# Query projections and key sums of two batches as one stretch of float32 products

## The chip, the cores and the metric

The kernel runs on one core of a Trainium2 chip. The metric is the device time of one execution in microseconds; smaller is better. TensorE (PE in the profile) multiplies matrices into PSUM, VectorE (DVE) and ScalarE (ACT) work elementwise and read PSUM, GpSimd (POOL) works on SBUF only, and SyncE (SP) issues all DMAs here. Each engine runs its instructions strictly in the order in which the program lists them.

## The reference

For each of 4 batches (4 heads, 1088 positions, head size 32) an attention with product features feeds a gated feed-forward block with a product over the positions. Everything is float32.

```python
def phi(x):                                   # S1, S2: 8 x 32
    a = einsum('rd,bhsd->bhsr', S1, x)
    b = einsum('rd,bhsd->bhsr', S2, x)
    return einsum('bhsi,bhsj->bhsij', a, b)   # 64 features a position and head
q_p, k_p = phi(q), phi(k)
kv = einsum('bhsf,bhsd->bhfd', k_p, v); z = k_p.sum(axis=2)    # sums over the keys
x = einsum('bhsf,bhfd->bhsd', q_p, kv) / (einsum('bhsf,bhf->bhs', q_p, z) + 1e-6)
h = relu(x @ w_in); u, v = h[..., :512], h[..., 512:]
v_n = (v - mean(v)) / sqrt(var(v) + 1e-6)
out = (u * (einsum('ts,bsd->btd', w_spatial, v_n) + b_spatial)) @ w_out
```

## The kernel before, in words

**Arithmetic.** The large products run as three passes on pairs of a high and a low part (type float32r, helper `mm3` at L444 to L446; `high` and `low` at L969, L971, L978 and L980). The small products of the attention run as plain float32: the projections of the keys (`project`, L593), the projections of the queries (`proj`, L733) and the sums over the keys (`part` in `keys`, L630). The profile shows a float32 product as two instructions. So a query group is 4 instructions (two halves of 192 or, in the last group, 160 columns), the keys of a batch are 36 with 64 columns, and the sums are 144 with 33 columns. The projections write 64 columns of the array, the sums 32.

**A batch's attention** (`attention(b)`, batches 1 to 3 counted from 0; batch 0 has its own path). Three query groups are loaded (`qt`, tag `c`), projected into a PSUM bank of tag `sd` each (`pab`), copied by ACT to `abT` (L737), written to DRAM (`qd`, L740) and read back in broadcast form (L744, L747) into `fa` and `fb` (tag `pl`); POOL multiplies these to query features (L748), which ACT and POOL split (tag `r`, L457). Meanwhile the keys are projected into two `sd` banks (`kab`); ACT copies one half to `ka` (L598) and DVE makes key features `kp` (L600), three buffers. The sums multiply those with the loaded values into another `sd` bank (`kv`), which DVE spreads to `kd` (L758) and ACT and DVE split to `kvh`, `kvl`. Then, for each of three groups: the numerators and denominators (`nd`, L775, three passes a piece), a reciprocal on DVE (L779), the attention's output `xh`, `xl`, and `hidden_v`, the half of the hidden layer that is normalised (`pv`, L799; tag `sd` again). Tag `sd` has two banks, and each tag hands out its buffers in the order in which the program creates the tiles. So the next batch's first projection follows the last `pv` of the batch before.

**Order of the work.** `main(b)` (hidden layer, product over the positions, output) and `attention(b + 1)` are interleaved by a planner: each operation has a planned cost and a due time worked back from the dues of what needs it, shifted by a table of corrections by name (`LEADS`). Among what could start in the planner's own clock, it takes the earliest due. `TURN = 125` is the planner's charge, in ns, for each change between float32 and float32r products (the flag `f4`). The planner yields one fixed order for each engine; on the chip, semaphores alone decide when an instruction starts. The last stage is `main(3)` with `quad`, which saves products by forming sums first.

Of the kernel before, what the change touches and what calls it, by code (L numbers as in the profile page):

```python
# [17 lines left out]
B, H, S, D, R = 4, 4, 1088, 32, 8  # L18
DM, DFF, DH = 128, 1024, 512
P = 128  # L20
# [12 lines left out]
TW = (384, 384, 320)  # L33
# [30 lines left out]
AFTER = (0, 35.0, 0, 0)  # L64
# [6 lines left out]
AFTER_T = 200.0  # L71
LAST = B - 1, ND - 1, 0
TAIL = (0, 212), (212, 212)

ON_ACT = ()
ADD_UP = 187
TURN = 125

SLACK = {'PE': 32, 'ACT': 56, 'DVE': 106, 'POOL': 890, 'SP': 84}

FILL_COLD, COLD_TO = 460, 7000
FILL, FILL_TO, FILL_SPARE = 224, 50.0, 150
FIRST_RATE, LOW_DELAY = 0.18, 4.4
# [50 lines left out]
class Order:  # L134
# [75 lines left out]
    def schedule(self):  # L210
# [31 lines left out]
        while left:  # L242
# [47 lines left out]
            if e == "PE":  # L290

                s += TURN * (o.f4 != f4)
                f4 = o.f4
# [56 lines left out]
def c_act(n, psum=False, ptr=False):  # L350
    return (157 if psum else 190) + 0.833 * n + (190 if ptr else 0) if n > 16 else 203
# [19 lines left out]
def tile_kernel(ctx: ExitStack, tc: tile.TileContext, kT, qT, vA, sks, idn, msk, wT, w_in, w_out, bsp, out):  # L371
# [6 lines left out]
    nc = tc.nc  # L378
# [57 lines left out]
    k = Order(place)  # L436
    k.whole = lambda tag: homes[tag].rearrange("p n c -> p (n c)")
    op, tl = k.op, k.tile

    def bank(tag, name):  # L440
        return tl(tag, name, [P, 512])
# [6 lines left out]
    def load(t, ap, src, kb, w=None, **kw):  # L448
        if t.name in FIRST:
            kw["due"] = FIRST.index(t.name) - 1e4  # L450
        op("SP", 470, lambda: nc.sync.dma_start(out=ap(), in_=src), w=[w or t], kb=kb, **kw)
# [9 lines left out]
    z9 = tl("u", "z9", [P, P])  # L461
# [3 lines left out]
    wps = bank("sd", "wps")  # L465
# [9 lines left out]
    eps = tl(None, "eps", [P, 2])  # L475
# [9 lines left out]
    NSK = 2 * H * R  # L485
# [44 lines left out]
    sk = tl(None, "sk", [P, 2 * NSK])  # L530
    s_raw = tl("pl", "s_raw", [P, 384])
# [5 lines left out]
    mask = tl(None, "mask_sb", [P, 2])  # L537
    load(mask, lambda: mask.ap, msk, 1)

    kd0 = tl("u", "kd0", [P, 2, 2, D + 1])  # L540

    wTh = tl(None, "wTh", [P, NS, ROW], F32R)
    wTl = tl(None, "wTl", [P, NS, ROW], F32R)
    wih = tl(None, "wih", [P, DFF], F32R)
    wil = tl(None, "wil", [P, DFF], F32R)
    woh = tl(None, "woh", [P, ND, DM], F32R)
    wol = tl(None, "wol", [P, ND, DM], F32R)
# [41 lines left out]
    def project(ab, xt, at=0):  # L589

        for t in range(3):
            for j in range(2):
                nc.tensor.matmul(ab_view(ab, at)[64 * j:64 * j + 64, :, t], xt[:, t * P + 64 * j:t * P + 64 * j + 64], sk[:, :NSK], start=True, stop=True)  # L593
# [19 lines left out]
    def keys(b):  # L613

        xts, vs = [], []
        for g in range(3):
            xt = tl("kt", f"kt{b}{g}", [P, 384])
            load(xt, lambda xt=xt, g=g: xt.ap, kT[b, g], 192, after=AFTER[b])
            v_sb = tl("v", f"v{b}{g}", [P, 3, H * (D + 1)])
            load(v_sb, lambda v_sb=v_sb: v_sb.ap.rearrange("p t c -> p (t c)"), vA[b, g], 198, after=AFTER[b])  # L620
            xts.append(xt)
            vs.append(v_sb)
        kv = bank("sd" if b else "pu", f"kv{b}")

        def part(g, f):
            for t in range(3):
                for pr in range(2):
                    for q in range(4):
                        c, h = 128 * pr + 32 * q, 2 * pr + q // 2
                        nc.tensor.matmul(  # L630
                            kv[32 * q:32 * q + 32, pr * (D + 1):(pr + 1) * (D + 1)], f[:, t, c:c + 32], vs[g][:, t, h * (D + 1):(h + 1) * (D + 1)],
                            start=(g == 0 and t == 0 and pr == 0), stop=(g == 2 and t == 2 and pr == 1), tile_position=(0, 32 * q),
                        )

        if not b:
            for g in range(3):
                f = phi(b, g, xts[g], "k")
                op("PE", 410, f4=True, fn=lambda g=g, f=f: part(g, f), r=[f, vs[g]], w=[kv])
            return kv

        abs_ = [bank("sd", f"kab{b}{n}") for n in range(2)]
        at = [(abs_[0], 0), (abs_[0], 192), (abs_[1], 0)]
        op("PE", 1058, f4=True, fn=lambda: [project(ab, xt, o) for xt, (ab, o) in zip(xts, at)], r=[*xts, (sk, "x")], w=abs_)
        fs = [features(b, g, at[g][0], "k", at[g][1]) for g in range(3)]
        op("PE", 1230, f4=True, fn=lambda: [part(g, fs[g]) for g in range(3)], r=[*fs, *vs], w=[kv])
        return kv

# [3 lines left out]
    def attention0(st):  # L651
# [17 lines left out]
        for g in range(3):  # L669
# [39 lines left out]
            op("PE", 330, f4=True, fn=x_turn, r=[x, ident], w=[xp])  # L709
            gs = slice(g * 384, (g + 1) * 384)  # L710
            op("ACT", c_act(384, True), lambda gs=gs, xp=xp: nc.scalar.copy(out=xh[:, gs], in_=xp[:, :384]), r=[xp], w=[(xh, g)])
            op("DVE", c_dve(384), lambda gs=gs, xp=xp: nc.vector.tensor_tensor(out=xl[:, gs], in0=xp[:, :384], in1=xh[:, gs].bitcast(F32), op=ALU.subtract), r=[xp, (xh, g)], w=[(xl, g)])
        st["lows"] = [tl("vl", f"vl{b}{d}", [P, NK, P], F32R) for d in range(ND)]
        for g in range(3):
            k.part = "h0", f"h0.{g}"
            hidden_v(b, st, g)

    def attention(b, st):
        x_tiles(b, st)
        xh, xl = st["xh"], st["xl"]  # L720

        fs = {}
        for g in range(3):
            k.part = "q", f"q{b}", f"q{b}.{g}"
            n = TW[g]
            xt = tl("c", f"qt{b}{g}", [P, 384])
            load(xt, lambda xt=xt, g=g, n=n: xt[:, :n], qT[b, g, :, :n], 192, after=AFTER[b])
            half = n // 2
            pab = bank("sd", f"pab{b}{g}")

            def proj(pab=pab, xt=xt, half=half):
                for x in range(2):
                    nc.tensor.matmul(pab[64 * x:64 * x + 64, :half], sk[:, :NSK], xt[:, x * half:x * half + half], start=True, stop=True)  # L733

            op("PE", 14 + 4 * half / 2.4, f4=True, fn=proj, r=[xt, (sk, "x")], w=[pab])
            ab = tl("abT", f"abT{b}{g}", [P, 192])
            op("ACT", c_act(half, True), lambda ab=ab, pab=pab, half=half: nc.scalar.copy(out=ab[:, :half], in_=pab[:, :half]), r=[pab], w=[ab])  # L737
            qd = tl("qd", f"qd{b}{g}", [NSK, 384])
            for x in range(2):
                op("SP", 630, lambda qd=qd, ab=ab, x=x, half=half: nc.sync.dma_start(out=qd[:, x * half:x * half + half], in_=ab[64 * x:64 * x + 64, :half]), r=[ab], w=[(qd, x)], kb=-half // 3)  # L740
            for pr in range(2):
                fa, fb = tl("pl", f"fa{b}{g}{pr}", [P, 384]), tl("pl", f"fb{b}{g}{pr}", [P, 384])
                r = 16 * pr
                op("SP", 640, lambda fa=fa, qd=qd, r=r, n=n: nc.sync.dma_start(out=fa[:, :n], in_=qd[r:r + 16, :n].unsqueeze(1).broadcast_to([16, R, n])), r=[qd], w=[fa], kb=-n // 3)  # L744
                for a in range(2):
                    at = 32 + r + 8 * a
                    op("SP", 640, lambda fb=fb, qd=qd, a=a, at=at, n=n: nc.sync.dma_start(out=fb[64 * a:64 * a + 64, :n], in_=qd[at:at + 8, :n].unsqueeze(0).broadcast_to([R, R, n])), r=[qd], w=[(fb, a)], kb=-n // 4)  # L747
                op("POOL", c_pool(n), lambda fa=fa, fb=fb, n=n: nc.gpsimd.tensor_tensor(out=fa[:, :n], in0=fa[:, :n], in1=fb[:, :n], op=ALU.mult), r=[fb], w=[fa])  # L748
                fs[g, pr] = fa
        k.part = "k", f"k{b}"  # L750
        kv = keys(b)
        kd = tl("kp", f"kd{b}", [P, 4, 2, D])
        for pr in range(2):
            for den in range(2):
                def part(pr=pr, den=den):
                    v = kv[:, pr * (D + 1):(pr + 1) * (D + 1)].unsqueeze(1)
                    src = v[:, :, D:].broadcast_to([P, 2, D]) if den else v[:, :, :D].broadcast_to([P, 2, D])
                    nc.vector.tensor_tensor(out=kd[:, 1 + pr if den else 3 * pr], in0=src, in1=mask.ap.unsqueeze(2).broadcast_to([P, 2, D]), op=ALU.mult)  # L758

                op("DVE", 215, part, r=[kv, mask], w=[(kd, (pr, den))])  # L760
        kvh, kvl = tl("kvh", f"kvh{b}", [P, 2, P], F32R), tl("kvl", f"kvl{b}", [P, 2, P], F32R)
        split(
            lambda: kvh.ap.rearrange("p r c -> p (r c)"), lambda: kvl.ap.rearrange("p r c -> p (r c)"), lambda: kd.ap.rearrange("p q a d -> p (q a d)"),
            256, [kd], [kvh], [kvl],
        )
        for g in range(3):
            k.part = "n", f"n{b}", f"n{b}.{g}"
            n = TW[g]
            x32, xn = tl("c", f"x32{b}{g}", [P, 384]), tl("c", f"xn{b}{g}", [P, 384])
            for pr in range(2):  # L770
                f = fs[g, pr]
# [624 lines left out]
```

## Time and profile before

| what | value |
| --- | --- |
| median of three runs | 328.0 us (327.64 to 328.73) |
| the profiled execution | 326.74 us |
| its span, first to last instruction | 325.0 us |
| granted TensorE clock, mean | 1.000 |
| PE busy | 318.4 us (98%) |
| DVE, ACT, POOL busy | 228.6, 166.1, 64.6 us |

Busy PE time is the union of overlapping matmuls, so it doesn't tell how tightly they follow one another. That is read from the starts in the order of time: two matmuls of 332 columns in a row start 0.15 us apart, and two of 512 columns 0.23 us.

### The profile page before, as it was taken

Reading aid. Unit: us, or ns where it says so; the run is one execution under the profiler, and the core shown is the slowest. Engines: PE = TensorE matmul, PEld = TensorE weight load, DVE = VectorE, ACT = ScalarE, POOL = GpSimd, SP = SyncE. Lnnn points to the kernel's source line nnn. Section 1 sums busy time; section 2 is a strip of 40 time slices with the busy share of each in tenths; the row PEclk is TensorE's granted clock in tenths of the full one; section 3 lists DMA queues with packets and bytes.
Section 4 is the critical chain, followed back from the end, with each engine's and each line's share of the span. In section 5 each row is a group of like instructions: output and inputs, shape, how many; then the busy total and the mean of one; then the engine's idle time right before and its main releaser. Section 6 shows DMA issues by size and latency. Waiting matters only on the chain.

```text
span 325.0 us, 6726 instructions
## 1 busy us (share of the span) xinstructions
PE 318.4 (98%) x2580; PEld 303.7 (93%) x2580; DVE 228.6 (70%) x513; ACT 166.1 (51%) x390; POOL 64.6 (20%) x81
## 2 busy tenths in 40 slices
PE   8899999999999999999999999999999999999995
PEld 7787999899999899999899999999999999999995
DVE  4799997646699973789986558897235697429382
ACT  2498667435774634566536457562314465416050
POOL 1000002486101026320103802150001321103000
PEclk9999999999999999999999999999999999999999
DMA  7832168854020274001034206001000321000001
GB/s 216 288 105 87 54 173 272 266 172 131 3 69 20 83 239 162 1 5 45 21 117 137 63 30 185 2 0 37 8 0 2 105 86 42 0 3 0 2 1 69
DMA packets 21548, 26.82 MB, mean 83 GB/s; under 512 B 2828, under 2 KB 21260, under 8 KB 21516
## 3 DMA queue, kind: packets, MB, share of 16 engines
q1 hardware_dynamic: 21516, 26.39, 26.2%
q8 instruction: 20, 0.33, 0.4%
q14 instruction: 12, 0.10, 0.1%
HBM read 23.31 MB, written 3.06 MB: 81 GB/s over the span
## 4 chain that ended last, share of the span: by engine, by line
PE 81%; DVE 8%; DMA 5%; ACT 3%; SPq 2%; issue 1%; ACTq 0%
PE sp L969 16%; PE sp L971 14%; PE sp L978 14%; PE sd L1203 4%; PE sp L1203 3%; PE sd L444 3%; PE sd L445 3%; PE sd L446 3%; PE pu L444 2%; PE po L445 2%; PE po L444 2%; DMA pl<-in_wT 2%; PE po L446 2%; PE sp L980 2%; PE pu L445 2%; PE pu L446 2%
## 5 line engine op out<-in xcount | busy, mean ns | idle before, releaser
L969 PE MATMUL sp<-wTh,vh 128*128 128x332 f32 (+1 forms) x350 | 114.8, 328 | 0.0
L971 PE MATMUL sp<-wTh,vl 128*128 128x332 f32 (+1 forms) x304 | 98.9, 325 | 0.0
L978 PE MATMUL sp<-wTl,vh 128*128 128x332 f32 (+1 forms) x304 | 97.0, 325 | 0.0
L969 PEld LDWEIGHTS sp<-wTh,vh 128*128 128x128 f32 x350 | 65.8, 188 | 2.2 <-issue 1.0
L971 PEld LDWEIGHTS sp<-wTh,vl 128*128 128x128 f32 x304 | 57.1, 188 | 0.6
L978 PEld LDWEIGHTS sp<-wTl,vh 128*128 128x128 f32 x304 | 57.1, 188 | 0.2
L454 DVE TENSOR_TENSOR g<-u,g 128x332 fp32r<-128x332 f32 (+1 forms) x41 | 24.3, 593 | 18.1 <-PE po L445 11.6
L523 ACT CAST g<-u 128x332 fp32r<-128x332 f32 (+1 forms) x41 | 19.8, 490 | 31.9 <-DVE u L1006 21.6
L1006 DVE TENSOR_TENSOR u<-sp,u 128x332 f32<-128x332 f32 (+1 forms) x43 | 22.3, 520 | 19.1 <-PE sp L980 12.6
L779 DVE RECIPROCAL c<-c 128x384 f32<-128x384 f32 (+1 forms) x9 | 21.8, 2419 | 16.0 <-ACT c L777 16.0
L961 ACT ACTIVATE u<-pu 128x332 f32<-128x332 f32 (+1 forms) x44 | 20.6, 469 | 22.0 <-PE pu L446 17.7
L882 ACT CAST vh<-vt 128x384 fp32r<-128x384 f32 x36 | 17.3, 511 | 20.6 <-DVE vt L841 11.6
L805 DVE BATCH_NORM_STATS2 st<-vt 128x6 f32<-128x512 f32 x36 | 24.0, 684 | 2.2 <-ACT vt L803 2.0
L748 POOL TENSOR_TENSOR pl<-pl,pl 128x384 f32<-128x384 f32 (+1 forms) x18 | 17.9, 1004 | 37.4 <-DMA pl<-qd 37.3
L457 POOL TENSOR_TENSOR r<-pl,r 128x384 fp32r<-128x384 f32 (+1 forms) x18 | 17.7, 988 | 36.8 <-ACT r L523 36.8
L803 ACT ACTIVATE vt<-sd 128x512 f32<-128x512 f32 x36 | 21.3, 603 | 7.1 <-PE sd L446 6.3
L884 DVE TENSOR_TENSOR vl<-vt,vh 128x384 fp32r<-128x384 f32 (+1 forms) x36 | 17.8, 505 | 5.3 <-ACT vh L882 5.2
L570 POOL TENSOR_TENSOR wTl<-pl,wTh 128x332 fp32r<-128x332 f32 (+1 forms) x9 | 8.2, 935 | 55.5 <-ACT wTh L567 52.6
L444 PE MATMUL pu<-xh,wih 128*128 128x332 f32 (+1 forms) x48 | 16.5, 344 | 0.4 <-ACT kp L961 0.2
L841 DVE TENSOR_SCALAR vt<-vt,mv,sm 128x512 f32<-128x512 f32 x33 | 16.7, 556 | 0.0
L567 ACT CAST wTh<-pl 128x332 fp32r<-128x332 f32 (+1 forms) x27 | 12.7, 499 | 7.1 <-DMA pl<-in_wT 6.9
L446 PE MATMUL pu<-xh,wil 128*128 128x332 f32 (+1 forms) x48 | 15.8, 329 | 0.0
(279 smaller groups left out, 641.6 us busy)
## 6 DMA issues: line engine op xcount, KB each, us to landing
pl<-in_wT SPq DMA_DIRECT2D x34, 166.0 KB
v<-in_vA SPq DMA_DIRECT2D x12, 198.0 KB
kt<-in_kT SPq DMA_DIRECT2D x12, 192.0 KB
pl<-qd SPq DMA_DIRECT2D x12, 192.0 KB
pl<-qd SPq DMA_DIRECT2D x24, 96.0 KB
pl<-in_wT SPq DMA_DIRECT2D x9, 212.0 KB
c<-in_qT SPq DMA_DIRECT2D x9, 192.0 KB
out<-u SPq DMA_DIRECT2D x6, 166.0 KB
```

The source lines that it names most:

```text
L444: nc.tensor.matmul(o, ah, bh, start=start, stop=False)
L445: nc.tensor.matmul(o, ah, bl, start=False, stop=False)
L446: nc.tensor.matmul(o, al, bh, start=False, stop=stop)
L454: return lambda: nc.vector.tensor_tensor(out=o(), in0=a(), in1=bb(), op=ALU.subtract)
L779: op("DVE", 135 + 6.3 * n, lambda x32=x32, n=n: nc.vector.reciprocal(out=x32[:, :n], in_=x32[:, :n]), w=[x32])
L803: op("ACT", c_act(512, True), lambda pv=pv, t=t: nc.scalar.activation(vt[:, t], pv.ap, AF.Relu), r=[pv], w=[(vt, t)])
L805: op("DVE", 690, lambda stats=stats, t=t: nc.vector.bn_stats(out=stats.ap, in_=vt[:, t]), r=[(vt, t)], w=[stats])
L969: nc.tensor.matmul(sp[:, :cw], vh[:, kt], wTh[:, kt, cs], start=(kt == begin), stop=False)
L971: nc.tensor.matmul(sp[:, :cw], vl[:, kt], wTh[:, kt, cs], start=False, stop=False)
L978: nc.tensor.matmul(sp[:, :cw], vh[:, kt], wTl[:, kt, cs], start=False, stop=False)
L1006: op("DVE", c_dve(cw), lambda: nc.vector.tensor_tensor(out=u.ap, in0=sp[:, :cw], in1=u.ap, op=ALU.mult), r=[sp], w=[u], lead=LEAD[1])
L1203: nc.tensor.matmul(x[:, :cw], p, q, start=i == 0 and n == 0, stop=end and i == 3 and n == 2)
```

## The change

It concerns batches 2 and 3 (`joint = b > 1`). `keys(b)` is called first, so the key and value loads, the two `kab` banks and the key features are created ahead of the query tiles. The sums are no longer an operation of their own: one operation projects the three query groups and then runs the 144 instructions of the sums. It needs the three query tiles, the key features and the values, and writes two `sd` banks in place of four: the first takes query groups 0 and 1 (columns 0 and 192), the second takes group 2 (column 0) and the sums (from column 192). No instruction of any engine is added or removed by this. Batch 1 keeps its separate operations.

The planner's costs change for batches 1 to 3: the keys from 1058 to 1110 ns, the sums from 1230 to 1850 ns. The joint operation is charged 1850 ns plus what the three projections were charged. `LEADS` has 94 names more and 1,382 changed values, from the normalisation of batch 0 (`vt02:4`) to the end, so the order of all engines is planned anew from there.

```diff
+C_KEYS, C_SUMS = 1110, 1850
...
 def keys(b):
...
-        op("PE", 1058, f4=True, fn=lambda: [project(ab, xt, o) for xt, (ab, o) in zip(xts, at)], r=[*xts, (sk, "x")], w=abs_)
+        op("PE", C_KEYS, f4=True, fn=lambda: [project(ab, xt, o) for xt, (ab, o) in zip(xts, at)], r=[*xts, (sk, "x")], w=abs_)
         fs = [features(b, g, at[g][0], "k", at[g][1]) for g in range(3)]
-        op("PE", 1230, f4=True, fn=lambda: [part(g, fs[g]) for g in range(3)], r=[*fs, *vs], w=[kv])
-        return kv
+        return [*fs, *vs], lambda kv: [part(kv, g, fs[g]) for g in range(3)]
...
 def attention(b, st):
...
+        joint = b > 1
+        if joint:
+            k.part = "k", f"k{b}"
+            kv_r, kv_sums = keys(b)
+            qts = [rows(g) for g in range(3)]
+            pabs = [bank("sd", f"pab{b}{n}") for n in range(2)]
+            places = [(pabs[0], 0), (pabs[0], 192), (pabs[1], 0)]
+            kv_bank = pabs[1]
+
+            def kv():
+                return kv_bank[:, 192:192 + 2 * (D + 1)]
+
+            def sums():
+                for xt, (pab, at), n in zip(qts, places, TW):
+                    proj(pab[:, at:at + n // 2], xt, n // 2)
+                kv_sums(kv())
+
+            op("PE", C_SUMS + sum(14 + 2 * n / 2.4 for n in TW), f4=True, fn=sums, r=[*qts, (sk, "x"), *kv_r], w=pabs)
...
-            op("PE", 14 + 4 * half / 2.4, f4=True, fn=proj, r=[xt, (sk, "x")], w=[pab])
+            if joint:
+                k.part = "q", f"q{b}", f"q{b}.{g}"
+                pab, at = places[g]
+            else:
+                xt, at = rows(g), 0
+                pab = bank("sd", f"pab{b}{g}")
+                op("PE", 14 + 4 * half / 2.4, f4=True, fn=lambda pab=pab, xt=xt, half=half: proj(pab[:, :half], xt, half), r=[xt, (sk, "x")], w=[pab])
...
-        kv = keys(b)
+        if not joint:
+            kv_r, kv_sums = keys(b)
+            kv_bank = bank("sd", f"kv{b}")
...
+            op("PE", C_SUMS, f4=True, fn=lambda: kv_sums(kv()), r=kv_r, w=[kv_bank])
```

## Rows read from the trace of the kernel before

**Rows 1.** The page: busy time of PE; its granted clock in 40 slices.

```profile
PE 318.4 (98%) x2580; PEld 303.7 (93%) x2580; DVE 228.6 (70%) x513; ACT 166.1 (51%) x390; POOL 64.6 (20%) x81
PEclk9999999999999999999999999999999999999999
```

**Rows 2.** Busy time by stage: stretch, PE, PEld, DVE, ACT, POOL, clock, DMA.

```profile
160.00:215.00 55.00, 55.00 (x488) 51.41 (x487) 40.49 (x88) 29.61 (x72) 15.04 (x17) 1.00 0.26 79
262.00:320.00 58.00, 58.00 (x359) 57.64 (x358) 35.60 (x85) 23.36 (x57) 7.61 (x12) 1.00 0.04 14
```

**Rows 3.** PE in order of time, query projections of batch 2: start, duration, instruction.

```profile
105.68 0.39 PE L445 MATMUL sd<-wil,xh 128*128 128x512 f32 x1
105.91 0.40 PE L446 MATMUL sd<-wih,xl 128*128 128x512 f32 x1
106.24 0.55 PE L733 MATMUL sd<-c,sk 128*64 128x192 f32 x4
...
106.97 0.32 PE L971 MATMUL sp<-wTh,vl 128*128 128x332 f32 x1
107.12 0.31 PE L978 MATMUL sp<-wTl,vh 128*128 128x332 f32 x1
107.36 0.82 PE L733 MATMUL sd<-c,sk 128*64 128x192 f32 x8
...
108.37 0.31 PE L971 MATMUL sp<-wTh,vl 128*128 128x332 f32 x1
```

**Rows 4.** PE in order of time around the sums of batches 2 and 3.

```profile
117.22 0.31 PE L446 MATMUL pu<-xh,wil 128*128 128x332 f32 x1
117.46 1.70 PE L630 MATMUL sd<-v,kp 128*32 128x33 f32 x144
...
119.35 0.31 PE L445 MATMUL pu<-xl,wih 128*128 128x332 f32 x1
...
170.95 0.32 PE L446 MATMUL pu<-xh,wil 128*128 128x332 f32 x1
171.20 1.96 PE L630 MATMUL sd<-v,kp 128*32 128x33 f32 x144
...
173.35 0.31 PE L445 MATMUL po<-g,woh 128*128 128x332 f32 x1
```

**Rows 5.** PE in order of time: projections and sums of batch 0; keys of batch 2.

```profile
7.41 0.57 PE L593 MATMUL sd<-sk,kt 128*64 128x64 f32 x12
7.90 0.63 PE L630 MATMUL pu<-v,kp 128*32 128x33 f32 x48
...
111.96 1.27 PE L593 MATMUL sd<-sk,kt 128*64 128x64 f32 x36
```

**Rows 6.** What PE's weight loads waited for after 20 us: total, times, longest.

```profile
PEld po L445 <- DVE xh L454: 0.8, 1, 0.8
PEld pu L444 <- ACT kp L961: 0.7, 2, 0.4
...
PEld pu L444 <- ACT u L961: 0.6, 3, 0.2
```

**Rows 7.** DVE in order of time: the key features of batch 2.

```profile
114.00 2.67 DVE L600 TENSOR_TENSOR kp<-ka,sd 128x768 f32<-128x768 f32 x3
```

**Rows 8.** POOL, then PE: query features split, and their first product (batch 2).

```profile
125.12 2.25 POOL L457 TENSOR_TENSOR r<-pl,r 128x384 fp32r<-128x384 f32 x2 [1.86 <-ACT r L523]
...
128.01 0.34 PE L444 MATMUL sd<-r,kvh 128*128 128x384 f32 x1
```

**Rows 9.** PE: last hidden-layer products of batches 2 and 3.

```profile
160.33 0.39 PE L446 MATMUL sd<-wih,xl 128*128 128x512 f32 x1
...
215.60 0.39 PE L446 MATMUL sd<-wih,xl 128*128 128x512 f32 x1
```

**Rows 10.** SyncE in order of time: the output stores of batches 1 and 2.

```profile
192.36 4.97 SPq L945 DMA_DIRECT2D out<-u  x3
...
266.67 6.44 SPq L945 DMA_DIRECT2D out<-u  x3
```

**Rows 11.** The page's costliest groups: the reciprocals (busy, mean ns).

```profile
L779 DVE RECIPROCAL c<-c 128x384 f32<-128x384 f32 (+1 forms) x9 | 21.8, 2419 | 16.0 <-ACT c L777 16.0
```

More of the change, by code (lines that the diff above doesn't have):

```diff
@@ L622, in keys, with part @@
             vs.append(v_sb)
-        kv = bank("sd" if b else "pu", f"kv{b}")
-        def part(g, f):
+        def part(kv, g, f):
             for t in range(3):
@@ L635, in keys @@
         if not b:
+            kv = bank("pu", f"kv{b}")
             for g in range(3):
                 f = phi(b, g, xts[g], "k")
-                op("PE", 410, f4=True, fn=lambda g=g, f=f: part(g, f), r=[f, vs[g]], w=[kv])
+                op("PE", 410, f4=True, fn=lambda g=g, f=f: part(kv, g, f), r=[f, vs[g]], w=[kv])
             return kv
@@ L720, in attention, with proj, rows @@
         xh, xl = st["xh"], st["xl"]
+        def proj(pab, xt, half):
+            for x in range(2):
+                nc.tensor.matmul(pab[64 * x:64 * x + 64], sk[:, :NSK], xt[:, x * half:x * half + half], start=True, stop=True)
+        def rows(g):
+            k.part = "q", f"q{b}", f"q{b}.{g}"
+            xt = tl("c", f"qt{b}{g}", [P, 384])
+            load(xt, lambda: xt[:, :TW[g]], qT[b, g, :, :TW[g]], 192, after=AFTER[b])
+            return xt
+        joint = b > 1
[13 more added lines that the diff above has]
+            op("PE", C_SUMS + sum(14 + 2 * n / 2.4 for n in TW), f4=True, fn=sums, r=[*qts, (sk, "x"), *kv_r], w=pabs)
@@ L722, in attention @@
         fs = {}
         for g in range(3):
-            k.part = "q", f"q{b}", f"q{b}.{g}"
             n = TW[g]
-            xt = tl("c", f"qt{b}{g}", [P, 384])
-            load(xt, lambda xt=xt, g=g, n=n: xt[:, :n], qT[b, g, :, :n], 192, after=AFTER[b])
             half = n // 2
[L729 to L733, printed above, removed]
@@ L735, in attention @@
-            op("PE", 14 + 4 * half / 2.4, f4=True, fn=proj, r=[xt, (sk, "x")], w=[pab])
+            if joint:
+                k.part = "q", f"q{b}", f"q{b}.{g}"
+                pab, at = places[g]
[3 more added lines that the diff above has]
+                op("PE", 14 + 4 * half / 2.4, f4=True, fn=lambda pab=pab, xt=xt, half=half: proj(pab[:, :half], xt, half), r=[xt, (sk, "x")], w=[pab])
             ab = tl("abT", f"abT{b}{g}", [P, 192])
-            op("ACT", c_act(half, True), lambda ab=ab, pab=pab, half=half: nc.scalar.copy(out=ab[:, :half], in_=pab[:, :half]), r=[pab], w=[ab])
+            op("ACT", c_act(half, True), lambda ab=ab, pab=pab, at=at, half=half: nc.scalar.copy(out=ab[:, :half], in_=pab[:, at:at + half]), r=[pab], w=[ab])
@@ L750, in attention, with kv @@
         k.part = "k", f"k{b}"
-        kv = keys(b)
+        if not joint:
+            kv_r, kv_sums = keys(b)
+            kv_bank = bank("sd", f"kv{b}")
+            def kv():
+                return kv_bank[:, :2 * (D + 1)]
+            op("PE", C_SUMS, f4=True, fn=lambda: kv_sums(kv()), r=kv_r, w=[kv_bank])
         kd = tl("kp", f"kd{b}", [P, 4, 2, D])
@@ L755, in part @@
                 def part(pr=pr, den=den):
-                    v = kv[:, pr * (D + 1):(pr + 1) * (D + 1)].unsqueeze(1)
+                    v = kv()[:, pr * (D + 1):(pr + 1) * (D + 1)].unsqueeze(1)
                     src = v[:, :, D:].broadcast_to([P, 2, D]) if den else v[:, :, :D].broadcast_to([P, 2, D])
                     nc.vector.tensor_tensor(out=kd[:, 1 + pr if den else 3 * pr], in0=src, in1=mask.ap.unsqueeze(2).broadcast_to([P, 2, D]), op=ALU.mult)
-                op("DVE", 215, part, r=[kv, mask], w=[(kd, (pr, den))])
+                op("DVE", 215, part, r=[kv_bank, mask], w=[(kd, (pr, den))])
         kvh, kvl = tl("kvh", f"kvh{b}", [P, 2, P], F32R), tl("kvl", f"kvl{b}", [P, 2, P], F32R)
```

2 lines of the change are left out of this document (1 added, 1 removed).

## The prediction, made before the changed kernel ran

> **What bounds the kernel now.** I read the page's busy shares first, then the busy time by stage, then PE's instructions in the order of time, last the waits. PE is busy 98% of the span at a clock that no slice shows below the full 2.4 GHz [rows 1]; the reader is to see that the clock can't be what changes. By stages PE has no idle time at all in 160 to 215 us and in 262 to 320 us, while DVE has some 15 us free in the one and 22 us in the other [rows 2]. So PE sets the end from the first quarter on, and a microsecond that PE no longer needs comes off the end, unless PE then waits for something it now finds ready. What busy time hides is the spacing. Two products of 332 columns start 0.15 us apart, two of 512 columns 0.23 us (105.68 to 105.91), and where a stretch of float32 products lies between float32r ones, the starts drift apart by more than the stretch itself [rows 3]. That excess is what the change can reach. Waits other than those are few: three groups of the list after 20 us that name another engine come to 0.8, 0.7 and 0.6 us, 2.1 us together [rows 6].
>
> **The change part by part.**
>
> *What a stretch costs.* A stretch's price is the time between the last float32r start before it and the second one after it, less the usual spacings. (The second, because the first one after a stretch is itself followed late: 106.71 to 106.97 where 0.15 is usual, inside the rows left out.) One query group alone: 105.91 to 106.97 is 1.06 us, less 0.23 and 0.15, leaves 0.68 us. Groups 1 and 2 together: 107.12 to 108.37 is 1.25 us, less twice 0.15, leaves 0.95 us [rows 3]. The second group of that pair (160 columns) so adds 0.95 - 0.68 = 0.27 us; by columns a group of 192 adds 0.27 x 192 / 160 = 0.32 us. A stretch therefore costs 0.68 - 0.32 = 0.36 us beside its products: entering and leaving. I call it a border. Batch 3 repeats both stretches within 0.01 us. The sums: 117.22 to 119.35 is 2.13 us, less 0.30, leaves 1.83 us in batch 2; 170.95 to 173.35, less 0.30, leaves 2.10 us in batch 3 [rows 4].
>
> *What goes.* Before, a batch has four stretches: group 0, groups 1 and 2, keys, sums. After, it has two: keys, and the joint one. Two borders a batch go: 2 x 0.36 = 0.72 us. The products stay: as many matmuls, of the same sizes. The keys' stretch stays as it is.
>
> *What comes.* Inside the joint stretch PE turns from projections (64 columns of the array) to sums (32 columns). No stretch of batches 1 to 3 has this seam, but the start of the kernel does: 12 instructions of the projections start at 7.41 and end 0.57 later; an instruction lasts 0.22 by itself, so the last began near 7.76. In the long stretch of 36 a pair starts every (1.27 - 0.22) / 17.5 = 0.06 us, so the next would have been due at 7.82; the sums start at 7.90 [rows 5]. The seam costs about 0.1 us. Bounds: 0 if that gap was a wait for data, and a whole border (0.36) at worst. I take 0.1, the only row that has the seam. The joint stretch then costs about 0.68 + 0.32 + 0.27 + (1.83 - 0.36) + 0.1 = 2.84 us in batch 2, where 0.68 + 0.95 + 1.83 = 3.46 us stood. That is 0.62 us a batch, 1.24 us for two.
> The Trainium skill, "TensorEngine Tiling (Array Packing)", Tiling Modes (Key Properties), says that changing the tiling mode, not merely the tile, drains the TensorE. The rows agree that there is something, at 0.1 us. Taken at its strongest, a drain as dear as a border, it would make the gain 0.36 us a batch; that is a rival below.
>
> *The sums' own spread.* The same 144 instructions took 1.83 and 2.10 us [rows 4], in neither case with an engine ahead that would explain the difference. Which of the two the joint stretches get, I can't read. Both at 1.83 would save 0.27 us more, both at 2.10 would cost 0.27 us. I take the mean, which is what stands there now.
>
> *Banks.* Four `sd` banks a batch become two in the later half, still two at a time, and the next taker (`nd`) comes many microseconds after. Nothing.
>
> *Moved: the query chain.* Keys first means that the queries now wait for the key features: from the keys' first product (111.96, [rows 5]) to the last feature (114.00 + 2.67 = 116.67, [rows 7]) is 4.7 us. So the projections of the queries, which began at 106.24 [rows 3], start about 5 us later within the batch; then come the same 6 writes and 18 broadcast reads on SyncE's queue, in the same number, and the same 6 products on POOL. The query chain is the later of the two today: the query features are split up to 127.37, and their first product starts at 128.01 [rows 8], while the sums were done at 119.2 [rows 4]. So the attention of batch 2 ends about 5 us later than at 160.6, and that of batch 3 about 10 us later than at 215.8 [rows 9]. I cost this at nothing. The cover is work of the main part: the stores of batch 1 end at 197.3, 36 us after its successor's attention is through, those of batch 2 at 273.1, 57 us after [rows 10, 9]. PE has that much to do meanwhile. Without the cover, the 5 or 10 us would come on top.
>
> *Moved: loads.* Key and value loads are now created ahead of the query loads. They are as many, and are issued far ahead of their use; nothing.
>
> *The new order.* The planner's sums go from 1230 to 1850 ns. With one TURN at each end (250 ns) the old plan had 1.48 us for a stretch that took 1.83 to 2.10, so the old order ran late against its clock by about half a microsecond after each sums; the new charge of 2.10 fits. That may take back some of the 2.1 us of waits [rows 6], and it may as well make new ones of the same size, since every queue is dealt anew from 30 us on. Between -1 and +1 us; I take nothing.
>
> **The sum.** The profiled execution: span 325.0 - 1.24 = 323.8 us, with the 1.74 us around it 325.5 us. The median of the runs is 1.26 us above that execution, so 328.0 - 1.2 = 326.8 us.
>
> **The rivals.** A change of less than 0.3% (1.0 us) is about what a measurement of this kernel can't tell from none.
>
> *A, the forecast: the borders go, PE hands the time to the end.* For it: PE without idle time [rows 2], the borders in four places at the same price. Against it: 1.2 us is little beside what a new order can move. Its own range is 325.8 to 327.4. Chance 0.58.
>
> *B, the seam is a border.* Turning from 64 to 32 columns in the middle costs as much as leaving and entering: gain 2 x (0.72 - 0.36) = 0.7 us, 327.3 us, within 0.3%. For it: the row has no seam between these very operations, as the queries of batches 2 and 3 (counted from 0) have three times the columns of the keys. Against it: 0.1 us at 7.8. This is also the strongest reading of the page's rule on tiling modes. Chance 0.18.
>
> *C, the gain is there and is given back.* The two stretches are shorter, but the new order has about a microsecond of new waits at other places, or the long stretch of 156 instructions runs at the dear end of the sums' spread. 327.5 to 328.3 us, no change to tell. Chance 0.15.
>
> *D, the joint stretch waits for the key features.* PE takes its instructions in order, so if the order puts the joint stretch ahead of the last feature on DVE, all of PE stands. Today the sums start 0.8 us after the last feature (116.67 to 117.46, [rows 7, 4]). One reciprocal of 2.42 us [rows 11] put ahead of the features on DVE would turn that into a wait of 1.6 us, in two batches 3.2 us: 328.0 - 1.2 + 3.2 = 330.0 us. It decides from waits of 2.2 us in all (1.2 of the gain, 1.0 of the resolution). Against it: the planner knows these costs well, and three groups of waits in 300 us are all that the old plan got wrong. Chance 0.09.
>
> **How the numbers follow.** The forecast is A's: 326.8 us. Faster by over 0.3% means below 327.0; A's own range goes over that line by a quarter, which C's and B's lucky ends make up for: 0.58. Slower by over 0.3% (above 329.0) is D: 0.09. The rest, 0.33, is within 0.3%. The range: below, 1.24 + 0.27 + 0.8 of waits regained = 2.3 us, 325.7; above, C's end at 328.3. D is left out.
>
> **What would show it.** Batches 2 and 3 each have two float32 stretches, 36 and 156 instructions long; the second, priced as above, takes 2.7 to 3.2 us; between the last L733 and the first L630 product the starts lie 0.1 us further apart than pairs do. Nothing but a 0.8 us margin lies between the last key feature and the joint stretch. The first `nd` product of a batch comes about 5 us later, counted from the first projection, and PE stays busy through it. PE has no idle time in 64 to 320 us, and the tail after the last product is the same. Wrong would be: an idle PE ahead of the joint stretch; a seam of 0.3 us; or a gain that comes mostly from elsewhere, the first 65 us or the quads.

## The result, and the profile after

The changed kernel took 329.65 us in the median of 20 runs (327.85 to 339.11), the kernel before 327.6 us on the same chip; the ratio is 1.0063, 95% interval 1.0041 to 1.0085. It is slower by 0.6%, where 326.8 us was predicted. (Some executions of either kernel were disturbed and came out several us longer; the medians here hold them, the ratios don't.) The profiled execution of after took 328.0 us, one of its quicker ones: span 326.2, against 325.0 before.

The page of after, PE's busy time and granted clock, answers to [rows 1]:

```profile
PE 318.0 (97%) x2580; PEld 303.0 (93%) x2580; DVE 225.6 (69%) x506; ACT 165.3 (51%) x390; POOL 70.5 (22%) x88
PEclk9999999999999999999999999999999999999999
```

The two stages of [rows 2], in after:

```profile
160.00:215.00 55.00, 54.89 (x495) 52.68 (x494) 41.68 (x87) 31.02 (x75) 15.32 (x17) 1.00 0.28 82
262.00:320.00 58.00, 57.66 (x356) 56.71 (x355) 35.24 (x82) 23.59 (x58) 9.92 (x16) 1.00 0.06 19
```

Clock and number of matmuls are the same, and PE is still the bound, but it now has idle time where it had none. The new plan also gives seven elementwise instructions to GpSimd that VectorE had (506 and 88 instructions, where 513 and 81 stood), so beside the order a little of the work changed engines. The stretches themselves did what was forecast and more. PE in order of time around the joint stretches of batches 2 and 3 (L723 projections, L629 sums), where before [rows 3, 4] had three stretches each:

```profile
112.27 0.35 PE L1009 MATMUL sp<-wTl,vh 128*128 128x424 f32 x1
112.55 1.14 PE L723 MATMUL sd<-c,sk 128*64 128x192 f32 x12
113.62 1.48 PE L629 MATMUL sd<-v,kp 128*32 128x33 f32 x144
115.03 0.43 PE L1000 MATMUL sp<-wTh,vh 128*128 128x332 f32 x1
115.30 0.31 PE L1002 MATMUL sp<-wTh,vl 128*128 128x332 f32 x1
...
176.15 0.31 PE L1009 MATMUL sp<-wTl,vh 128*128 128x332 f32 x1
176.39 1.14 PE L723 MATMUL sd<-c,sk 128*64 128x192 f32 x12
177.46 1.43 PE L629 MATMUL sd<-v,kp 128*32 128x33 f32 x144
178.83 0.42 PE L1000 MATMUL sp<-wTh,vh 128*128 128x332 f32 x1
179.09 0.32 PE L1002 MATMUL sp<-wTh,vl 128*128 128x332 f32 x1
```

Priced as in the prediction: 115.30 - 112.27 less 0.19 (spacing at 424 columns) and 0.15 is 2.69 us; 179.09 - 176.15 less 0.30 is 2.64 us. Before, the same work cost 0.68 + 0.95 + 1.83 = 3.46 us in batch 2 and 0.67 + 0.94 + 2.10 = 3.71 us in batch 3. PE needs 0.77 + 1.07 = 1.84 us less. So the loss lies elsewhere. What PE's weight loads waited for after 20 us answers to [rows 6]:

```profile
PEld po L446 <- DVE xh L455: 0.8, 1, 0.8
PEld sd L447 <- DVE xl L455: 0.8, 1, 0.8
PEld pu L445 <- ACT u L992: 0.8, 3, 0.4
...
PEld pu L445 <- ACT kp L992: 0.7, 2, 0.4
PEld po L446 <- DVE xl L455: 0.7, 1, 0.7
PEld sp L1000 <- DVE u L1037: 0.7, 1, 0.7
...
PEld po L446 <- DVE g L455: 0.6, 2, 0.4
```

Seven groups of 0.6 us or more name another engine. Before there were four: the three shown in [rows 6], and 0.7 us for abT ahead of the projections (L733), among the lines left out there. At this size the waits for xl (twice), for g and for u out of sp are new.

The waits can be added up from the matmul starts: outside the float32 stretches and the start right behind each (which is in the stretch's price), every distance between two starts beyond the usual spacing (0.15, 0.19 and 0.23 us at 332, 424 and 512 columns) is time lost, and a shorter one is taken off again; the sums are good to about 0.2 us. "Stretches" is the price of those of batches 2 and 3 without the keys. All in us, each row from one profiled execution; the labels are those of the experiments below.

```
                    span   stretches  40-65  65-106 106-160 160-215 215-262 262-322  lost
before              325.0    7.17      0.9     0.2     0.4     0.7     0.0     0.5    2.8
after               326.2    5.33      1.4     0.2     0.7     0.6     1.0     1.0    4.9
e1 after again      326.9    5.32      1.9     0.1     0.7     2.1     1.0     1.0    6.8
e2 old to 94        325.7    5.32      0.3     0.3     0.7     2.0     1.0     0.9    5.3
e3 new to 70        326.5    6.80      1.4     0.3     0.3     0.8     0.1     0.6    3.5
e4 old to 52        327.5    5.32      1.5     0.1     0.7     2.1     1.0     1.0    6.4
e5                  325.6    5.33      1.8     0.0     0.8     1.1     0.7     1.1    5.4
e6                  325.8    5.33      1.3     0.1     0.8     0.7     1.4     0.4    4.7
e7                  325.8    5.33      0.9     0.3     0.8     0.7     1.4     0.3    4.3
e8 stretch broken   329.7    5.74      2.1     1.9     0.5     2.2     1.0     1.0    8.7
e9                  325.2    5.33      0.0     0.6     0.8     1.7     0.5     0.9    4.5
e10 before, mended  324.6    7.18      0.4     0.3     0.3     0.8     0.1     0.7    2.4
e11 after, mended   323.7    5.32      0.5     0.7     0.4     0.5     0.3     0.5    2.8
e12                 322.6    5.33      0.0     0.2     0.4     0.8     0.3     0.4    2.0
```

For the second run of after the account closes: 5.32 - 7.17 + 6.8 - 2.8 = +2.2 us, and its span is 1.9 us longer. (The first 20 us differ from one execution to the next, in either kernel: PE's 300th product starts at 19.4 us in the profile of before, at 20.3 in the first of after and at 18.9 in e1. So spans compare within about a microsecond, stretches and losses better.)

### The profile page after: what moved, and what is told of

The parts are those of the page before. It is cut to its first block, busy times and chain, and to the rows that moved or that the text cites. A ratio compares the mean times of both kernels' runs of the same rounds, so it can differ in the third digit from the quotient of the medians.

```text
span 326.2 us, 6714 instructions
## 1 busy us (share of the span) xinstructions
PE 318.0 (97%) x2580; PEld 303.0 (93%) x2580; DVE 225.6 (69%) x506; ACT 165.3 (51%) x390; POOL 70.5 (22%) x88
## 4 chain that ended last, share of the span: by engine, by line
PE 70%; DVE 15%; ACT 5%; DMA 4%; issue 3%; SPq 1%; POOL 1%; DVEq 0%; POOLq 0%; ACTq 0%
PE sp L1000 13%; PE sp L1002 11%; PE sp L1009 11%; PE sd L1234 4%; DMA pl<-in_wT 4%; PE sp L1234 3%; PE sd L445 3%; PE sd L447 3%; PE sd L446 3%; PE po L446 2%; PE pu L445 2%; PE po L447 2%; PE sp L1011 2%; PE pu L446 2%; PE pu L447 2%
## 5 line engine op out<-in xcount | busy, mean ns | idle before, releaser
L772 POOL TENSOR_TENSOR pl<-pl,pl 128x384 f32<-128x384 f32 (+1 forms) x18 | 18.8, 1052 | 50.4 <-DMA pl<-qd 50.3
L455 DVE TENSOR_TENSOR g<-u,g 128x332 fp32r<-128x332 f32 (+1 forms) x41 | 22.7, 553 | 9.7 <-PE po L446 5.3
L601 DVE TENSOR_TENSOR kp<-ka,sd 128x768 f32<-128x768 f32 x15 | 13.8, 950 | 5.3 <-ACT ka L599 2.6
```

Source lines behind the costliest of these rows:

```text
L455: return lambda: nc.vector.tensor_tensor(out=o(), in0=a(), in1=bb(), op=ALU.subtract)
```

## The experiments

In e2 to e13 the order of every engine and the buffers are written out as a list taken from the kernels' own plans, then edited. Plans "before" and "after" replayed that way give the kernels' own order. The list sits ahead of the kernel's code, so the same line has a higher number there.

**e1 to e4: which part of the new order loses.** e1 is the changed kernel once more. e2 and e4 take the order of before up to 94 or 52 us of planned time and then that of after, with joint stretches; e3 takes the order of after up to 70 us and then that of before, with the stretches apart.

```diff
-order = plan("after")
+order = plan("before")[start < 94 us] + rest of plan("after")     # e2; e4: 52 us
+order = plan("after")[start < 70 us] + rest of plan("before")     # e3, joint = False
```

> The changed kernel itself, again, beside the others on one chip. In the shown profiles the two joint stretches cost 2.69 and 2.63 us where the separate ones cost 3.46 and 3.71, so 1.84 us of PE were saved, and yet the time rose by 0.6%. Both theories expect a ratio of 1.004 to 1.009 to the kernel before, the stretches again at 2.6 to 2.8 us, and some 3 to 4 us of PE waits or later data elsewhere, at places that this second profile should show again: 63 to 66 us, 199, 216 and 269 us. A wait that is not there again was chance.

> All engines' instructions that the old plan starts before 94 us (of the planner's clock; about 98 us on the chip) stand in the old order; behind them comes the new order with the joint stretches. Theory 1, the loss lies in the new order of 40 to 70 us, where ACT's casts of gate products are queued behind casts of weight pieces that DMA brings: the ratio falls to 0.994 to 0.998, as the 1.8 us saved come through less some 1 us of late waits, and the waits at 63 to 66 us are the old kernel's 0.6 us. Theory 2, the loss lies behind 100 us, in the waits around the later attention (199, 216, 269 us): the ratio stays at 1.004 to 1.008.

> The reverse: the new order of all engines up to 70 us of the planner's clock, then the old order to the end, with the queries and the sums in separate stretches as before. Theory 1: slower than before, 1.004 to 1.009. Theory 2: no change, 0.999 to 1.001.

> As the old-to-94 kernel, but the old order ends at 52 us of the planner's clock; the new order of 52 to 94 us stays. If theory 1 holds and the harm is done in 40 to 52 us (other order of weight loads and of the first products over the positions), this gives 0.994 to 0.998; if it is done in 52 to 70 us (gate products behind the third column piece's casts), 1.004 to 1.008. Theory 2: 1.004 to 1.008.

Against the kernel before (327.41 us here): e1 329.09 us, 1.0038 (1.0012 to 1.0064); e2 328.41, 1.0033 (1.0009 to 1.0056); e3 329.24, 1.0044 (1.0014 to 1.0074); e4 329.9, 1.0061 (1.0035 to 1.0087). Both theories are half right, and e2 lies in neither one's range. e3 has nothing of the joining, and is slower all the same: in its profile the new order costs some 0.5 us between 40 and 65 us by itself, which is less than half of what its median lost; the rest isn't laid to a place. e2 is free of the early loss and still loses some 2.7 us more than before behind 160 us. e4 has the early loss as well, so it comes from the order of 52 to 94 us.

**e5: one late wait.** In e1 PE stands 1.36 us at 190. VectorE, GpSimd and PE of e1 in order of time:

```profile
188.35 2.41 POOL L772 TENSOR_TENSOR pl<-pl,pl 128x384 f32<-128x384 f32 x2 [22.23 <-DMA pl<-qd]
188.52 2.52 DVE L915 TENSOR_TENSOR vl<-vt,vh 128x384 fp32r<-128x384 f32 x2
190.96 0.49 DVE L1037 TENSOR_TENSOR u<-sp,u 128x332 f32<-128x332 f32 x1
191.51 0.42 PE L1000 MATMUL sp<-wTh,vh 128*128 128x332 f32 x1 [1.20 <-DVE u L1037]
```

The same place in the first profile of after, where GpSimd came half a microsecond after VectorE instead of before it:

```profile
189.21 0.89 DVE L915 TENSOR_TENSOR vl<-vt,vh 128x384 fp32r<-128x384 f32 x2
189.74 2.53 POOL L772 TENSOR_TENSOR pl<-pl,pl 128x384 f32<-128x384 f32 x2 [22.94 <-DMA pl<-qd]
190.01 0.50 DVE L1037 TENSOR_TENSOR u<-sp,u 128x332 f32<-128x332 f32 x1
```

Two splits of VectorE take 2.52 us when GpSimd's products of batch 3's query features begin first, 0.89 us when they begin after; the product u, which reads PSUM and one tile of SBUF, takes 0.50 us beside the same GpSimd products. PE waits for u only in the first case. GpSimd's two products took 2.41 and 2.53 us here, and 2.00 at 180 us in the kernel before, where VectorE did nothing beside them: both sides pay. The Trainium skill, "SBUF — State Buffer", Who interferes with whom, says that a VectorE instruction with two SBUF inputs contends with a GpSimd instruction that reads SBUF, that one with at most one SBUF input (outside the two-port modes) does not, and that who issues first decides who blocks: the rows agree, with 2.52 against 0.89 us for the two inputs and 0.50 and 0.49 us for u. e5 changes VectorE's order alone:

```diff
 DVE order, 189 us
+  u (out of sp), g low
   vl, vl
-  u (out of sp)
   vl, vh
-  g low
```

> The changed kernel with one edit: on VectorE the two products that a hidden tile and the gate behind the wait at 190 us hang on (u out of sp, and g's low part) go ahead of four splits of normalised values (vl, vh out of vt) that nothing needs before 240 us. In the run before (the changed kernel again) two of those splits took 2.52 us because they lay beside GpSimd's products of query features (pl, 2.41 us), where alone they take 0.89; the product u came out late and TensorE stood 1.36 us at 190. Theory 1 (the loss is a handful of TensorE's waits behind late results, and an order without them has none): the wait at 190 is gone, no other wait of TensorE grows, span 325.3 to 325.8 and a median near 327.7 to 328.2, that is 0.3 to 0.4% under the changed kernel. Theory 2 (another engine is the bound in this stretch and the wait only shows it): the splits or the gate come late instead, over 0.8 us of waiting turns up between 190 and 215, and the median stays within 0.15% of the changed kernel's, 329.1.

327.87 us, 1.0029 (1.0007 to 1.0051; the kernel before took 327.23 us beside e5 to e8). The wait is gone, as PE's starts at the place show:

```profile
189.80 0.35 PE L621 MATMUL pu<-xh,wil 128*128 128x424 f32 x1
189.98 0.31 PE L1174 MATMUL sp<-wTh,vh 128*128 128x332 f32 x1
```

GpSimd's products take 2.00 us there, and the three splits behind them 1.35. The loss of 160 to 215 us falls from 2.1 to 1.1 us, the total from 6.8 to 5.4, and nothing between 190 and 215 us takes the wait's place. Theory 1 holds for this place by the profile; the medians alone (1.0038 to 1.0029) could not tell it from no change.

**e6 and e7: four more edits.** e6 adds the others to the order of after, e7 has them behind the order of before up to 94 us.

```diff
 PE order, 119 and 199 us:  one po, one pu   -> a group later
 DVE order, 214 us:   -  t, tw, t, xl        +  xl, t, tw, t
 DVE order, 268 us:   -  wo, g low, wo, u    +  u, wo, g low, wo
```

> The changed kernel with the edit of the run above and four more of the kind, each on one engine and by one to four places: the matmuls of the waits at 119 (first po of the second gate) and at 199.5 (third pu) one matmul group later on TensorE; the low part xl of batch 3's second query group ahead of two small normalisation steps and of a weight's product on VectorE (wait at 216 to 218); the product u ahead of a gate's low part and two weight splits on VectorE (wait at 269). The early part, up to 100 us, stays as in the changed kernel. The waits sum to 0.28 + 1.36 + 0.27 + 0.82 + 0.50 = 3.2 us with some 0.1 us behind each for the start of the next group. Theory 1: all go, span 323.2 to 324.2, median 325.5 to 326.3, faster than the kernel before by 0.3 to 0.6%. Theory 2 (the waits move on): TensorE's lost time behind 100 us stays over 3 us and the median above 327.7.

> The old order of all engines up to 94 us, then the changed kernel's, with the five edits of the run above. If early and late losses are separate and add up, this has the joint stretches' gain of 1.84 us, none of the waits at 119, 190, 199, 216 and 269 and only the old kernel's waits near 63: span 322.5 to 323.3, median 324.8 to 325.6, 0.6 to 0.8% faster than the kernel before. Theory 2: over 327.5.

e6: 328.21 us, 1.0029 (1.0006 to 1.0052); e7: 326.47 us, 0.9979 (0.9955 to 1.0003). e6 missed its forecast by 2 us and e7 its own by 0.9; e6's loss behind 106 us, 3.3 us, is on theory 2's side. The waits at 190 and 269 went. At 119 I had moved another po than the one that waits; at 199 the wait moved one pu on (0.27 to 0.40); and at 216 the two waits of 0.52 and 0.19 became one of 0.98. In e7, ScalarE and PE there in order of time:

```profile
216.97 0.47 ACT L698 CAST g<-u 128x332 fp32r<-128x332 f32 x1 [2.51 <-DVE u L1211]
217.47 1.09 ACT L1008 ACTIVATE vt<-sd 128x512 f32<-128x512 f32 x2
...
218.12 0.50 PE L619 MATMUL sd<-wih,xh 128*128 128x512 f32 x1 [0.82 <-ACT vt L1008]
```

PE, no longer held by xl, now needs the bank that ScalarE is to empty (vt), and ScalarE stands in its own queue before a gate's cast, which waits for VectorE's u. A wait mended on one engine showed the next engine's.

**e8: the stretch broken.** One group of three products that ran ahead of the joint stretch runs between projections and sums; nothing else changes place.

```diff
 PE order
-  sp group, [projections + sums]
+  [projections], sp group, [sums]
```

> The changed kernel in its own order, but the joint stretch of each of the two batches is broken in two: one group of three column-wide matmuls (sp, 424 columns) that ran just ahead of the stretch now runs between the projections and the sums. All engines keep their order otherwise, the buffers too. Theory 1 (the saving lies in the uninterrupted stretch): each break costs one border less the seam, 0.36 - 0.10 = 0.26 us, or up to 0.76 to 1.08 us if the short gaps inside the sums come back too: 0.5 to 1.8 us in all, median 329.6 to 330.9. Rival (the saving came from neighbours and buffers, not from joining): the pieces of the broken stretch sum to the joint one's 2.69 and 2.63 us within 0.1 us, and the median stays within 0.3 us of the changed kernel's 329.1.

PE of e8 in order of time, batch 2:

```profile
113.42 0.35 PE L1183 MATMUL sp<-wTl,vh 128*128 128x424 f32 x1
113.70 1.14 PE L897 MATMUL sd<-c,sk 128*64 128x192 f32 x12
114.77 0.46 PE L1174 MATMUL sp<-wTh,vh 128*128 128x424 f32 x1
115.07 0.35 PE L1176 MATMUL sp<-wTh,vl 128*128 128x424 f32 x1
115.26 0.35 PE L1183 MATMUL sp<-wTl,vh 128*128 128x424 f32 x1
115.54 1.49 PE L803 MATMUL sd<-v,kp 128*32 128x33 f32 x144
116.95 0.43 PE L1174 MATMUL sp<-wTh,vh 128*128 128x332 f32 x1
117.22 0.31 PE L1176 MATMUL sp<-wTh,vl 128*128 128x332 f32 x1
```

The projections cost 115.07 - 113.42 - 0.37 = 1.28 us, the sums 117.22 - 115.26 - 0.34 = 1.62; batch 3 has 1.27 and 1.57. Joint, both cost 2.69 and 2.63: a break costs 0.21 us a batch, close to the 0.26 forecast, and the sums are as short alone as joined. The median, 331.28 us (ratio 1.0113, 1.0073 to 1.0153), is 2 us more than that explains, and can't be laid to the break: the profile lost it between 62 and 69 us, ahead of the edit (last section). It is not that one execution's: the mean granted clock was 0.995 in the profile, and 0.98 to 0.998 in the five others. Why, with an order that is the same up to there, is open.

**e9 to e12: the early place, and all places.** Between 61 and 64 us ScalarE has weight casts (wTh) that wait for their loads, and gate casts behind them. ScalarE of after in order of time:

```profile
61.83 0.94 ACT L568 CAST wTh<-pl 128x332 fp32r<-128x332 f32 x2 [0.80 <-DMA pl<-in_wT]
62.68 0.54 ACT L524 CAST xh<-kp 128x424 fp32r<-128x424 f32 x1
63.12 0.46 ACT L568 CAST wTh<-pl 128x332 fp32r<-128x332 f32 x1
63.49 0.54 ACT L524 CAST xl<-kp 128x424 fp32r<-128x424 f32 x1
```

and PE's products that need their results:

```profile
64.26 0.46 PE L446 MATMUL po<-xh,woh 128*128 128x424 f32 x1 [0.53 <-DVE xh L455]
...
65.47 0.46 PE L446 MATMUL po<-xl,woh 128*128 128x424 f32 x1 [0.38 <-DVE xl L455]
```

Behind the gate cast at 60.56 (of another tile), the plan of before has one weight cast ahead of xh, the plan of after two, and PE has one group less to do ahead of the products. In the edit below, xh and xl are g cast 1 and 2. e9 makes only this edit in after, e10 the like in before. e11 has after's order with all places mended (VectorE's g low at 118; ScalarE's u at 199 and vt at 217, in place of the two PE edits that missed), e12 the same behind the order of before up to 94 us.

```diff
 ACT order, 61 us
+  g cast 1
   wTh
+  g cast 2
   wTh
-  g cast 1
   wTh
-  g cast 2
```

> The changed kernel with one edit on ScalarE alone: two casts of gate products (g, 424 columns) go ahead of two casts of weight pieces that wait for their loads until 61 to 62 us. In the changed order two such weight casts stand ahead of the first gate cast, in the order before one; TensorE's waits at 62 to 65 us are 0.72 + 0.54 us with two restarts of 0.11, up to 2.1 us of lost time between 40 and 65 us in other runs of it. Theory 1 (the early loss is that place in ScalarE's queue): those waits are gone, lost time between 40 and 65 us under 0.6 us, median 1.2 to 1.6 us under the changed kernel's 329.1: 327.5 to 327.9. Rival (the late loads themselves hold TensorE, the casts' place doesn't matter): the waits stay within 0.3 us.

> The kernel before with the same kind of edit: on ScalarE three gate casts go ahead of the weight casts that wait for their loads at 61 us. The kernel before loses 0.62 us there with two restarts of 0.11. Theory 1: lost time between 40 and 65 us falls from 1.2 to about 0.4 us, median 326.6 to 326.8, 0.2% under the kernel before. It says how much of the next two runs' gain isn't the change's. Rival: no difference over 0.3 us.

> The changed kernel's own order with the edit of e9 and the late ones mended better than in e6: gl (VectorE) ahead of two splits at 118; the products u and gl ahead of four splits at 189; the activation u (ScalarE) ahead of a cast of query features that waits for GpSimd at 198.8; xl (VectorE) ahead of small normalisation steps and, new, the eviction of the attention's result (vt, ScalarE) ahead of a gate cast at 217; u ahead of splits and gl at 269. Theory 1 (the loss is these waits and nothing else): lost time outside the float32 stretches falls to 0.6 between 40 and 65, 0.6 between 106 and 160, 0.5 between 160 and 215, 0.3 between 215 and 262, 0.4 behind: some 3.5 us under the second run of the changed kernel, median 325.3 to 326.0, faster than before by 0.4 to 0.7%. Theory 2 (the waits only move on): above 327.3.

> The order before up to 94 us with the edit of e10, then the changed order with the late edits of e11. Stretches 1.84 us shorter and waits as few as in e10: theory 1 has it 1.8 us under e10, 324.8 to 325.3, 0.7 to 0.9% under the kernel before, and equal to e11 within 0.4 us. Theory 2: no faster than e7's 326.5.

Against before at 327.29 us: e9 328.38 us, 1.0022 (1.0002 to 1.0043); e10 326.58, 0.9978 (0.9964 to 0.9991); e11 325.64, 0.9952 (0.9936 to 0.9968); e12 324.35, 0.9911 (0.9893 to 0.9929). In e9, ScalarE's gate cast comes first:

```profile
60.72 0.55 ACT L704 CAST xh<-kp 128x424 fp32r<-128x424 f32 x1
61.63 0.47 ACT L748 CAST wTh<-pl 128x332 fp32r<-128x332 f32 x1 [0.36 <-DMA pl<-in_wT]
62.00 0.54 ACT L704 CAST xl<-kp 128x424 fp32r<-128x424 f32 x1
```

The loss of 40 to 65 us is gone, though a wait of 0.51 us appears at 66.7; the late places stay, and the median gains 0.7 us on e1, half of what I expected and within what the intervals leave open. The loads are as late as before, so their lateness alone doesn't hold PE; the casts' place does. e11 and e12 came out as theory 1 had it, e12 below its range and 1.3 us below e11, where I expected them within 0.4 us of each other.

e10 is the fairest measure of the joining here: with waits mended in both (in e10 the early ones alone, as its order has no late one above 0.2 us), e12 is 2.2 us faster than e10. By the two profiles 7.18 - 5.33 = 1.85 us of it are the stretches, 0.4 us fewer waits.

**e13: the gaps inside the sums.** Before, the 144 instructions ran with short gaps, and DMA traffic lay beside them; in the joint stretches neither was there. e13 adds traffic to e12.

```diff
+for _ in range(3 if b == 3 else 0):      # SyncE, beside batch 2's joint stretch
+    for g in range(3):
+        load(xts[g], lambda g=g: xts[g].ap, kT[b, g], 192, after=AFTER[b])
```

> The kernel of e12 with work added: SyncE issues the three key loads of batch 3 three times more, one round after the other, so that DMA traffic lies beside batch 2's joint stretch, where there was none. Theory 3 (the short gaps of 0.05 to 0.14 us inside the sums go with DMA traffic: the sums took 1.83 and 2.10 us with DMA shares of 0.89 and 0.60 beside them before, and 1.6 us with shares of 0.00 and 0.04 in the joint stretches): gaps of over 50 ns come back among the 144 instructions and batch 2's joint stretch costs 2.85 to 3.2 us where it cost 2.69; batch 3's, with nothing added, stays at 2.63. Rival (the gaps come from something else): 2.69 within 0.03 us though the DMA share there is over 0.3. The later chain of batch 2's queries, issued behind these loads, may cost time of its own; the median is no test.

Busy time by stage in e13, the projections and the sums of the joint stretch (last columns: clock, DMA share, GB/s):

```profile
118.50:119.60 1.10, 1.10 (x13) 0.77 (x12) 1.10 (x7) 0.47 (x1) 0.00 (x0) 1.00 0.70 210
119.60:121.20 1.60, 1.60 (x147) 1.52 (x146) 1.60 (x5) 0.00 (x0) 0.00 (x0) 1.00 0.63 179
```

The starts before and after the stretch give its price, 121.31 - 118.28 less 0.34:

```profile
118.28 0.35 PE L1193 MATMUL sp<-wTl,vh 128*128 128x424 f32 x1
...
121.31 0.31 PE L1186 MATMUL sp<-wTh,vl 128*128 128x332 f32 x1
```

With a DMA share of 0.6 to 0.7 the stretch cost 2.69 us, as without. My theory of the gaps fell, at least for these loads. (The one execution took 336.91 us, 12.6 more than e12. 8.1 us of that were lost before the joint stretch, most of it in the first 40 us, where the granted clock was 0.82 and then 0.75; the other 4.6 at 126 to 134 us, where the queries' transfers stood behind the added loads and PE waited 2.9 us.)

What the traces do show is a coincidence. Beside the sums of every joint stretch and of e8's broken ones, all without gaps, ScalarE and GpSimd did next to nothing; beside all sums with gaps of over 0.05 us, in every run, one of the two was at work for a quarter of the time or more. No run tests whether that is the cause.

## Why the prediction was wrong

**What bounds the kernel: right.** PE still sets the end, and what it loses comes off or on the end: e11 and e12 show it in one direction, e1 in the other.

**The border, 0.36 us: right.** Three projections in one stretch cost 1.28 us (e8) where two stretches cost 0.68 + 0.95 = 1.63 us: one border, 0.35 us. **The seam, 0.1 us: right** by the starts (0.23 us from the last projection pair to the first sums, where pairs of 160 columns start 0.13 apart), and by e8's 0.21 us for a break. The borders and the seam alone gave 0.35 + 0.21 us in batch 2 and 0.34 + 0.21 in batch 3, 1.11 us where 1.24 was forecast. Rival B, a seam as dear as a border, would have made a break free; it fell, and with it the strongest reading of the Trainium skill's rule in "TensorEngine Tiling (Array Packing)", Tiling Modes (Key Properties). **Rival D** didn't occur: in batch 2 the last key feature ends at 109.27 + 2.69 = 111.96 and the joint stretch begins at 112.55; in batch 3 it is 175.94 and 176.39.

**The sums' own spread: mis-sized.** I took what stood there, 1.83 and 2.10 us. They run in 1.62 and 1.57 us in their new place, joined or not (e8), which is 0.21 + 0.53 = 0.74 us of gain that has nothing to do with borders. That the stretches gained 1.84 us where 1.24 was forecast is luck, then. What makes the gaps, I don't know; loads alone don't (e13).

**"I cost this at nothing", the query chain: failed in part.** It is later than I worked out: batch 2's first product of query features starts at 138.03 (before 128.01, [rows 8]), batch 3's at 195.72 (before 179.84), and the last hidden-layer products at 169.87 and 229.19 (160.33 and 215.60, [rows 9]): 9.5 and 13.6 us later, where I had 5 and 10. Apart from the waits named here PE did have work meanwhile, as I argued. But room in the due time isn't all: GpSimd's first two products of batch 3's query features, which ran at 171.6 to 173.8 us before, now run at 188 to 192 us, beside VectorE's splits, and the wait of 1.36 us is the price (e5). The waits at 199 and 216 to 218 hang on the same later chain: 1.36 + 0.27 + 0.52 + 0.19 = 2.3 us in all. That they would not be there without the joining is argued, not shown: no run has the new order behind 94 us with the stretches apart.

**"The new order. Between -1 and +1 us; I take nothing": this step failed.** PE lost 2.1 us more than before in the first profile and 4.0 us in the second. It is rival C with a wrong size: its upper end took "about a microsecond" of new waits, when the new plan held six new ones of 0.2 to 0.5 us in the first profile and eight of 0.2 to 1.4 us in the second. The old plan's waits were no measure of what a new one would have, and the prediction also counted three groups, 2.1 us, where the list behind [rows 6] has a fourth of 0.7 us. e3 (0.44% slower, without joining), e9, e11 and e12 show that the loss lies in the order of the queues, and that mending a few places in it takes it back.

## What to carry to other kernels

A saving of 1 to 2 us on the bounding engine is real only after the order of the others has been looked at: where a change makes a planner deal every queue anew, several new waits can cost more than the change gains. Mend such waits one at a time in the queue of the engine that is late, not on the engine that waits, and look again: of the first five edits two removed their wait, the two on PE's own order gained nothing, and one only showed the next engine's queue. And replay the old order as far as it goes, so that gain and order can be told apart.

## What the runs showed of the hardware

**In e8 and e13 the granted clock fell after PE had waited.** In e8 PE waited 1.17 and 0.79 us between 62.5 and 64.9 us, and the start at 66.05 came another 0.50 us late, when the clock was already falling. The granted clock by stage in e8:

```profile
60.00:64.00 4.00, 2.98 (x20) 2.71 (x18) 1.54 (x4) 1.89 (x5) 0.56 (x1) 1.00 0.95 286
64.00:66.00 2.00, 1.41 (x4) 0.54 (x4) 1.99 (x3) 1.48 (x4) 1.47 (x2) 0.82 0.33 100
66.00:69.00 3.00, 2.95 (x11) 2.90 (x12) 1.73 (x2) 1.06 (x3) 2.68 (x3) 0.55 0.51 183
69.00:75.00 6.00, 6.00 (x117) 5.79 (x116) 2.08 (x3) 2.19 (x5) 4.00 (x5) 1.00 0.45 142
```

In finer stretches it was 1.00 until 65, 0.64 from 65 to 66 and 0.50, that is 1.2 GHz of 2.4, from 66 to 68.6. From 66.05 on PE runs without a pause, and products of 332 columns start 0.28 us apart in place of 0.15. That adds about 1.3 us to the waits. In e13 the same follows the wait of 2.9 us at 128: the clock is 0.60 in 132 to 134 us. In after and e1, with waits of 1.3 and 1.7 us in all at 62 to 66, it stayed at 1.00.

**A wait costs a little more than its length.** Behind PE's waits for another engine the second product started some 0.11 us late: in after, 0.11 us behind each of the waits at 63.4, 64.8, 118.9, 199.5, 215.6, 217.6 and 268.8.
